# One list scheduler for a whole arm of an mLSTM and top-1 expert kernel

## The chip, the cores and the metric

The kernel runs on one core of a Trainium2 chip. A core has five engines with a queue each, which work in order and wait for each other on semaphores: TensorE (PE, with its weight loads shown apart as PEld), VectorE (DVE), ScalarE (ACT), GpSimd (POOL) and SyncE (SP), which here issues nearly all DMAs. The metric is the device time of one execution in microseconds; a smaller one is better.

## The reference

Two layers follow one another. The first is an mLSTM over 4 batches, 8 heads and 768 steps with head size 40. Each head keeps a 40 x 40 matrix state:

```python
m_new = np.maximum(f_gate[:, :, t] + m, i_gate[:, :, t])
f_stab = np.exp(f_gate[:, :, t] + m - m_new)
i_stab = np.exp(i_gate[:, :, t] - m_new)
C = f_stab * C + i_stab * outer(vt, kt)
n = f_stab * n + i_stab * kt
y[:, :, t] = sigmoid(o_gate[:, :, t]) * (C @ qt) / maximum(abs(n @ qt), 1)
```

The second takes the 3072 rows of 320 numbers and sends each to one of 8 experts, the one with the largest `x @ w_gate + modality_bias[modality_id]`; its output is `gate_w * (relu(x @ w1[e]) @ w2[e])` with a hidden size of 1024. All data is fp32. The large products are made of fp16 high and low parts.

## The kernel before

**Units.** The sequence is cut into 24 units, a batch and 128 steps each. `begin` computes the gates and a flag that says whether the state still moves after the first 128 steps of a batch; where it doesn't, the arm `still_state` runs, as it does in the runs shown, and otherwise the arm `general`. In `still_state` the first unit of each batch is "heavy": exponents on PE (`e`), their exp on ACT, scores on PE (`s`), and the product on DVE; it also gives the batch's state (`kw` on POOL, `up` on PE, `bd` on DVE). The other 20 units are "light": one product of q with the state (`values_l`). Every unit then has a denominator (`den`, DVE), an output gate (`so`, POOL; the logistic function before it, `sig`, is three ACT steps per half batch), the product (`row`, DVE), a sum of absolute values for scaling (`sum`, ACT) and an indirect store to the DRAM table `x_d` (`store`, POOL).

**Tiles.** The store puts a row where its modality says: rows of modality 0 from the front, those of modality 1 from the back. So 256 rows in a row ("tile") have one modality, and nearly all of them want the expert that the modality's bias alone would choose. Twelve such tiles go through that guessed expert (`deal`, six per modality, the weights of both kept on chip). A tile is loaded from `x_d` (SP), scaled and split into fp16 parts ("columns", ACT and DVE), turned by a DMA transpose (SP), and multiplied: layer 1 is four groups of 16 matmuls (`p`), each with a ReLU into a high part (`hh`, ACT) and a low part (`hl`, DVE); layer 2 is two halves of 128 rows with 24 matmuls each (`o`), a scaling (ACT) and an indirect store of the output (POOL). The first two tiles need five units, the next two nine, and so on.

**Gates, lists, rest.** The true logits of a tile are computed as well (`verify`, 16 small matmuls and some DVE steps). Rows that want another expert are masked in the output and put on lists in DRAM (`lists`). `work_list` turns these into "rest" tiles, of which two with 128 rows are done at the end (`slots`), with other weights: loaded, split into fp16 parts by ACT (`high`) and DVE (`low`), and the rows gathered by an indirect DMA.

**What sets the order.** The program order is written by hand (`manual_schedule`). Up to the second tile it comes from the class `Order`: tasks with an engine, a cost in us, what they come after, and the buffers they take; `give` walks forward in time, on each engine takes the task that can start first (within 0.2 us, the one with the longest way to the end), and emits the code in that order. It holds 12 units, the columns of four tiles, the weights of the two guessed experts, and the first two tiles; `FILL` warm-up matmuls go into PE's idle time. All the rest is done by eight generators ("threads") that `together` lets do one step each in turn, once per half of a quarter of a tile's matmuls (a half-beat): `light` (the 12 other units), `load_work`, two `column_work`, `weight_work`, `verify_work`, `list_work`, `rest_work`. Between them they wait for counts of half-beats, such as

```python
while now - max(turned[k, j] for k in range(NMOD) for j in js) < 2:
    yield
```

A thread that gives DVE more work than `FULL` elements in one half-beat makes patient threads wait (`Meter` counts them). The two rest tiles come after all threads are done.

Lines that the text below names: 1165 layer 1 on PE, 1169 and 163 its `hh` and `hl` (all DVE instructions carry line 163, the `Meter`'s), 1194 layer 2, 966 the output store, 943 the load of a tile, 997 the transpose, 954 the gather, 1667 `so`, 574 `store`, 1678 and 1685 the read-out of light and heavy units, 456 and 441 scores and exponents, 881 and 886 the weights' loads, 899 their `high`.

## Time and profile before

| | us |
|---|---|
| three runs | 280.53, 282.58, 283.46 |
| their median | 282.58 |
| the profiled execution | 280.47 |
| its span, first to last instruction | 278.8 |
| PE busy | 244.7 |
| DVE, ACT, POOL busy | 163.4, 126.9, 97.0 |

The mean granted TensorE clock is 0.952 of full speed. 41.20 MB go through the DMA engines, most of them in the first 90 us. In the profile a row of the groups reads: line, engine, operation, output <- inputs, shapes, count, then the busy time in us and the mean of one in ns, then the engine's idle time before such instructions and what ended it. A row of the timeline reads: start and length in us, engine, line, operation, and in square brackets the idle time before it and what ended that. A tile's busy time on PE can be read from the matmuls' starts; single matmuls overlap.

### The profile page before, as it was taken

The numbers are of one execution on the slowest core, as the hardware profiler recorded it, in microseconds if no ns is written. First come the engines' busy times: TensorE is split into PE (matmuls) and PEld (weight loads), VectorE is DVE, ScalarE is ACT, GpSimd is POOL, SyncE is SP. The second block draws the span as 40 slices with busy tenths as digits, with TensorE's granted clock in tenths as the row PEclk, the third lists the DMA queues.
The fourth block names the chain that finished last, engine by engine and source line by source line (L and its number), as shares of the span: only waits on it lengthen the run. The fifth ranks groups of instructions, "written<-read, shape, count | busy, mean of one in ns | idle before, by whom it ended". The sixth has DMA issues, their size and how long they took to land. (4 is left out here: it accounts for less than half of the span.)

```text
span 278.8 us, 6063 instructions
## 1 busy us (share of the span) xinstructions
PE 244.7 (88%) x2191; PEld 198.5 (71%) x2191; DVE 163.4 (59%) x572; ACT 126.9 (46%) x230; POOL 97.0 (35%) x159
## 2 busy tenths in 40 slices
PE   8984968999889999999999998999999989919930
PEld 3554854987768988879788886888787858708820
DVE  5886855885781465754857277656454756863200
ACT  4687562768742163824624353523131326772200
POOL 8275642253644136254453704021112214110110
PEclk9999587999999999999999999999999999986995
DMA  4985876997848004793351728881000068891000
GB/s 150 304 263 133 224 279 222 226 310 288 278 112 230 32 25 136 218 153 106 101 143 45 198 56 195 137 162 46 26 26 23 25 201 273 241 286 24 3 12 1
DMA packets 36666, 41.20 MB, mean 148 GB/s; under 512 B 23879, under 2 KB 27945, under 8 KB 36626
## 3 DMA queue, kind: packets, MB, share of 16 engines
q1 hardware_dynamic: 33650, 32.46, 43.2%
q0 software_dynamic: 2688, 8.23, 8.8%
q8 instruction: 19, 0.31, 0.5%
q14 instruction: 21, 0.17, 0.2%
q10 hardware_dynamic: 288, 0.03, 0.1%
HBM read 27.57 MB, written 8.55 MB: 130 GB/s over the span
## 5 line engine op out<-in xcount | busy, mean ns | idle before, releaser
L1165 PEld LDWEIGHTS <-wx 128*128 128x128 f16 x896 | 83.7, 100 | 18.5 <-DMA sg<-xr 7.1
L1194 PE MATMUL o_ps<-wx,hh 128*128 128x320 f16 x416 | 85.5, 299 | 0.0
L1165 PE MATMUL h_ps<-xT,wx 128*128 128x256 f16 x576 | 66.5, 272 | 2.3 <-DVE hl L163 2.3
L163 DVE SCALAR_TENSOR_TENSOR hl<-h_ps,hh 128x512 f16<-128x512 f32 x52 | 35.6, 687 | 50.6 <-ACT hh L1169 50.2
L1194 PE MATMUL o_ps<-wx,hl 128*128 128x320 f16 x208 | 62.2, 299 | 1.1 <-DVE hl L163 1.1
L1169 ACT ACTIVATE hh<-h_ps 128x512 f16<-128x512 f32 x52 | 30.8, 593 | 46.5 <-PE h_ps L1165 46.5
L1194 PEld LDWEIGHTS <-hh 128*128 128x128 f16 x416 | 39.9, 98 | 14.0
L966 POOL DMA_INDIRECT out<-ob,oi x24 | 25.1, 1045 | 69.3 <-ACT ob L965 65.1
L1667 POOL TENSOR_TENSOR so<-sg,den 128x320 f32<-128x320 f32 x24 | 20.5, 853 | 47.2 <-DVE den L163 39.5
L163 DVE SCALAR_TENSOR_TENSOR wx<-ws,wx 128x768 f16<-128x768 f32 (+1 forms) x24 | 27.8, 1157 | 11.8 <-ACT wx L899 11.5
L965 ACT ACTIVATE ob<-o_ps,entall 128x320 f32<-128x320 f32 x24 | 12.5, 523 | 46.6 <-PE o_ps L1194 38.7
L574 POOL DMA_INDIRECT x_d<-row,place_i x24 | 24.5, 1023 | 12.2 <-ACT ya L571 3.2
L1194 PEld LDWEIGHTS <-hl 128*128 128x128 f16 x208 | 20.3, 98 | 9.6 <-DVE hl L163 1.8
L899 ACT ACTIVATE wx<-ws 128x768 f16<-128x768 f32 (+1 forms) x24 | 23.3, 977 | 5.8 <-DMA ws<-in_w 5.8
L1678 PE MATMUL y_ps<-wx,eb 80*128 80x82 f32 x160 | 22.3, 288 | 2.4 <-DVE row L163 2.4
L1678 PEld LDWEIGHTS y_ps<-wx,eb 80*128 80x128 f32 x160 | 21.0, 206 | 3.1 <-issue 2.8
L1314 PE MATMUL warm_ps<-warm 128*128 128x512 bf16 x57 | 17.1, 464 | 6.0 <-DVE ah L163 3.6
L1165 PE MATMUL h_ps<-eb,wx 128*128 128x256 f16 x192 | 21.4, 273 | 0.0
L1314 PEld LDWEIGHTS <-warm 128*128 128x128 bf16 x57 | 6.5, 116 | 15.2 <-issue 10.3
L542 ACT ACTIVATE sg<-sg 128x960 f32<-128x960 f32 x16 | 15.8, 995 | 0.8 <-DMA sg<-in_og 0.7
L163 DVE SCALAR_TENSOR_TENSOR ex<-xg,sc,ex 128x64 f16<-128x64 f32 (+1 forms) x44 | 14.4, 378 | 0.9 <-ACT ex L989 0.9
L163 DVE TENSOR_TENSOR row<-y_ps,so 128x320 f32<-128x320 f32 x24 | 11.6, 482 | 5.5 <-POOL so L1667 5.5
(246 smaller groups left out, 259.0 us busy)
## 6 DMA issues: line engine op xcount, KB each, us to landing
ws<-in_w SPq DMA_DIRECT2D x16, 384.0 KB, 4.8
ws<-in_w SPq DMA_DIRECT2D x8, 640.0 KB, 7.7
xg<-x_d SPq DMA_DIRECT2D x14, 322.0 KB, 3.0
sg<-in_og SPq DMA_DIRECT2D x8, 480.0 KB, 5.5
eb<-in_ql SPq DMA_DIRECT2D x8, 320.0 KB, 5.7
kt<-in_kv SPq DMA_DIRECT2D x4, 324.0 KB
wx<-in_qk SPq DMA_DIRECT2D x8, 160.0 KB
eb<-in_ql SPq DMA_DIRECT2D x4, 160.0 KB, 2.3
```

Of the source, the lines that this page charges most:

```text
L163: return op(out, *args, **kw)
L542: nc.scalar.activation(t, t, AF.Exp, scale=-1.0)
L574: ins = nc.gpsimd.indirect_dma_start(out=x_d[:, :], out_offset=bass.IndirectOffsetOnAxis(ap=place_i[:, n:n + 1].bitcast(U32), axis=0), in_ ...
L899: nc.scalar.mul(halves[p][0], pieces[p], WSC)
L965: nc.scalar.mul(ob, o_ps, fac)
L966: disjoint("out", nc.gpsimd.indirect_dma_start(out=out[:, :], out_offset=bass.IndirectOffsetOnAxis(ap=oi.bitcast(U32), axis=0), in_=ob, in ...
L1165: nc.tensor.matmul(h_ps[:, i], lhsT=l, rhs=r, start=(i == 0 and q == 0), stop=(i == g - 1 and q == 7), skip_group_check=True)
L1169: nc.scalar.activation(hh[:, f0:f0 + g, 0:n], made[f0], AF.Relu)
L1194: nc.tensor.matmul(o_ps, lhsT=l[:, fc, hs], rhs=r[:, fc], start=(fc == 0 and a == 0), stop=(fc == NFC - 1 and a == 2))
L1314: nc.tensor.matmul(ps, lhsT=warm[:, 0:P], rhs=warm, start=True, stop=True, skip_group_check=True)
L1667: nc.gpsimd.tensor_tensor(sos[n], sgs[n // SGH][:, n % SGH].rearrange("p (h d) -> p h d", h=H), dens.pop(n).broadcast_to([P, H, D]), ALU.mult)
L1678: nc.tensor.matmul(y_ps[:, 2 * p:2 * p + 2], lhsT=qat[n][0:2 * D, p], rhs=bds[n // NCH][0:2 * D, p], start=(p == 0), stop=(p == NP - 1), s ...
```

## The change

`Order` now holds everything that the arm does: all 24 units, the columns of the twelve tiles and of the two further ones that are only verified, their gates and lists, the work list, the rest rows' gather, columns and weights, and all fourteen tiles; `first_work` becomes `all_work`, `first_tile` becomes `add_tile`, and the threads, the half-beats and the `Meter` are gone. These parts are changed with it:

- A task's way to the end counts the hop between engines (`HOP`, and `DEEP` behind PE), an added distance (`more`), order-only relations (`then`) and hints. Costs and latencies have new values. Only SP's DMAs wait for the modelled DMA line.
- Layer 1 of a tile comes after layer 1 of the tile before it and layer 2 of the one before that, so it may go ahead of the previous tile's layer 2. From the third tile on its groups go through the banks `psS`, `psS`, `psM`, `psS` where two `psS` banks (later `psS` and `psG`) served before.
- The first eight units use the banks of `psG` and `psS` by turns; before, all used the two of `psG`.
- Output scaling and output store are separate tasks (`scaled`, `send`).
- The idle filler is 12 matmuls of 128 columns (`keep_warm`, into a corner of a bank in use) at 0.8 us distance, until the first tile; before, 4 of 512 columns.
- `begin` now also issues a q group, the second half of the gates of batch 0 and the step constants, and does POOL's remaining constants, the padding and a zeroing that the arm did.

```diff
-FILL = 4
+FILL = 12
...
-    HOP = 0.12
+    HOP = 0.15
+    DEEP = 0.3
     NEAR = 0.2
-    WRITTEN = 2.2
-    LANDED, RATE = 1.7, 300e3
-
+    LANDED, RATE = 2.1, 300e3
     AHEAD = 0.7
...
+    def give(self, loaded, line, idle):
+
+
+        order, _, last = self.forth(loaded, line, idle, self.ways(loaded))
+        for _, _, do in order:
+            if do:
+                do()
+
+    def ways(self, loaded):
+
+        behind, then = ({n: [] for n in self.all} for _ in range(2))
+        for n, t in self.all.items():
+            for d, i in ((behind, "after"), (behind, "hint"), (then, "then")):
+                for a in t[i]:
+                    if a not in loaded:
+                        d[a].append(n)
         way = {}
 
         def back(n):
             if n not in way:
                 t = self.all[n]
-                way[n] = 0.0
-                way[n] = t["c"] + t["lag"] + (t["size"] / self.RATE + self.LANDED if t["size"] else 0) + max(
-                    [back(m) for m in behind[n]], default=0.0)
+                way[n] = t["c"] + max([back(m) for m in then[n]] + [
+                    t["lag"] + t["more"] + (t["size"] / self.RATE + self.LANDED if t["size"] else 0.0) +
+                    max([back(m) + self.hop(n, m) for m in behind[n]], default=0.0)])
             return way[n]
 
-        behind = {n: [] for n in self.all}
-        for n, t in self.all.items():
-            for a in t["after"]:
-                if a not in loaded:
-                    behind[a].append(n)
         for n in self.all:
             back(n)
-        free, end, line = {}, dict(loaded), 0.0
+        return way
+
+    def hop(self, a, b):
+        a, b = (self.all[n]["e"] if n in self.all else "" for n in (a, b))
+        return 0.0 if a == b else self.DEEP if a == "PE" else self.HOP
...
-                at = max([free.get(t["e"], 0.0)] + [end[a] + (self.HOP if engine.get(a) != t["e"] else 0) for a in t["after"]])
-                if t["size"]:
+                at = max([free.get(t["e"], 0.0)] + [end[a] + self.hop(a, n) for a in t["after"]])
+                if t["size"] and t["e"] == "SP":
...
+    def keep_warm(count):
+
+        ps = ubank[:, 512 - P:]
+        for _ in range(count):
+            nc.tensor.matmul(ps, lhsT=warm[:, 0:P], rhs=warm[:, 0:P], start=True, stop=True, skip_group_check=True)
...
+        pad_qk(1)
+        run_all(more_constants())
...
+        load_ql(0, 3, 2)
+        sgs.append(load_o(1))
+        load_steps_c(0)
...
+            for i, n in enumerate(U):
+
+                y, bank = (("s", (psS, "s")) if i < 8 and i % 2 else ("g", (psG, "g")))
                 r = [x for x, (b, c, k) in enumerate(qgroups) if b * NCH + c <= n < b * NCH + c + k]
                 if n % NCH:
-                    add(f"v{n}", "PE", 0.95, lambda n=n: values_l(n), [f"bd{n // NCH}", f"q{r[0]}"], [("g", f"row{n}")])
+                    add(f"v{n}", "PE", 0.95, lambda n=n, bank=bank: values_l(n, bank), [f"bd{n // NCH}", f"q{r[0]}"], [(y, f"row{n}")])
                 else:
-                    add(f"v{n}", "PE", 1.8, lambda n=n: values_h(n), [f"w{n},0", f"w{n},1"] + ([f"kv{n // NCH}"] if n else []), [("g", f"row{n}")])
+                    add(f"v{n}", "PE", 1.8, lambda n=n, bank=bank: values_h(n, bank), [f"w{n},0", f"w{n},1"] + ([f"kv{n // NCH}"] if n else []), [(y, f"row{n}")])
...
+                add(f"store{n}", "POOL", 1.05, lambda n=n: store_x(n), [f"sum{n}", "place"], size=165e3)
...
+            free_w = ([], ["s12,0", "s12,1", "s18,0", "s18,1"], all_v + [f"e{NCH * b},{hf}" for b in range(B) for hf in range(2) if b or hf],
+                      [f"o{done},1,1"])
...
+            head = deal + [(k, NST) for k in range(NMOD)]
...
+                    [f"store{n}" for n in range(UNITS[j])] + (["plan2"] if x else []), [("xg", f"xl{x},1")], 330e3,
+                    more=10.0 if x > 1 else 0.0)
+                add_columns(x, tl, [f"load{x}"] + ([f"sc{x - 1}"] if x else []), NH)
...
+            for i, js in enumerate(sets):
+                g, ls = verify(gs[i], js[0] == NST), lists(gs[i])
+                xs = [head.index((k, j)) for k in range(NMOD) for j in js]
+                big = len(js) > 1
+                for y, x in enumerate(xs):
+                    add(f"lg{x}", "PE", 0.5, lambda g=g: next(g), [f"xt{x},{h}" for h in range(NH)] +
+                        ([f"lg{xs[y - 1]}"] if y else ["wgr"] + ([f"gate{i - 1},0"] if i else [])))
+                for d, c in enumerate((1.5, 1.6, 1.0) if big else (1.2, 1.25, 0.8)):
+                    add(f"gate{i},{d}", "DVE", c, lambda g=g: next(g), [f"gate{i},{d - 1}"] if d else [f"lg{xs[-1]}", "plan4"] +
+                        ([f"gate{i - 1},2"] if i else []) + ([f"list{i - 2},2"] if i > 1 else []))
+                for d, (e, c) in enumerate((("DVE", 0.8), ("PE", 0.3), ("DVE", 1.3), ("DVE", 1.0), ("POOL", 1.7))):
+                    add(f"list{i},{d}", e, c, lambda ls=ls, d=d: (next(ls), next(ls) if d == 0 else 0), [f"list{i},{d - 1}"] if d else
+                        [f"gate{i},2"] + ([f"list{i - 1},3"] if i else []), lag=3.5 if d == 4 else 0.0, more=3.0 if d == 1 else 0.0)
+                if i == 0:
+                    w.all["list0,4"]["after"].append("zeros")
...
+            for x, (k, j) in enumerate(deal):
+                add_tile(w, x, early_w[k], tls[k, j], k, f"gate{[j in js for js in sets].index(True)},2", x > 1)
+
+            gt = []
+            for q, (wts, tl) in enumerate(slots):
+                x = len(head) + q
+
+                def lists_of(q=q, tl=tl):
+                    gt.append(gather_steps(rest, (0, TS)[q], tl, 1))
+                    next(gt[q])
+
+                add(f"load{x}", "SP", 1.7, lists_of, ["work3"] + [f"list{i},4" for i in range(n_sets)] + ([f"load{x - 1}"] if q else []), size=10e3)
+                add(f"rows{x}", "POOL", 1.7, lambda q=q: next(gt[q]), [f"load{x}"], [("xg", f"xl{x},0")], 165e3)
+                add_columns(x, tl, [f"rows{x}", "work5"], 1, lambda q=q: run_all(gt[q]))
+                add_tile(w, x, wts, tl, 2 + q, "work5", True, 1)
+            loaded = {"q0": 0.0, "w0,0": 0.0, "o0": 0.0, "get0,0": 0.5, "get0,1": 1.8, "q1": 3.4, "o1": 5.4, "steps0": 6.7}
+            w.give(loaded, 4.8, (lambda: keep_warm(FILL), 0.06 * FILL, 0.8, "p0,0"))
...
+        def add_tile(w, x, wts, tl, k, gates, more, nh=NH):
+
+            hid, made, l1, obs = [], {}, {}, {}
+            names = "ssms" if more else "s"
+            pools = [dict(s=(psS, "s"), m=(psM, "misc"))[i] for i in names]
+            n = NW1 * nh // NH
+
+            order = list(w.last)
+            after = [f"p{c},{w.last[c][0]}" for c in order[-1:]] + [f"o{c},{w.last[c][1]},1" for c in order[-2:-1]]
 
             def layer(part, f0):
                 if not l1:
-                    l1.update(zip("gphl", layer1_parts(wts, tl, both, hid, h_pools[0:1])))
+                    l1.update(zip("gphl", layer1_parts(wts, tl, list(range(nh)), hid, pools)))
                 l1[part](f0)
 
             def second(h, i):
                 made[h] = layer2_part(wts, hid, h, i, made.get(h))
-                if h and i:
-                    used(tl)
-
-            for i in range(NW1):
-                f0 = i * NFC // NW1
-                w.add(f"p{x},{i}", "PE", 1.78, lambda f0=f0: layer("p", f0), [f"low{x},{i}"] + [f"xt{x},{h}" for h in range(NH)] +
-                      ([f"p{x},{i - 1}"] if i else [f"o{x - 1},1,1"] if x else []) + (["gate4"] if (x, i) == (1, 0) else []), [("s", f"hl{x},{i}")])
+
+            for i in range(n):
+                f0, z = i * NFC // n, NW1 // n
+
+                w.add(f"p{x},{i}", "PE", 1.78, lambda f0=f0: layer("p", f0), [f"low{k},{c}" for c in range(z * i, z * i + z)] +
+                      [f"xt{x},{h}" for h in range(nh)] + ([f"p{x},{i - 1}"] if i else after),
+                      [(names[i % len(names)], f"hl{x},{i}")])
+                if order and i == n - 1:
+                    w.all[f"o{order[-1]},0,0"]["hint"].append(f"p{x},{i}")
                 w.add(f"hh{x},{i}", "ACT", 0.62, lambda f0=f0: layer("h", f0), [f"p{x},{i}"])
                 w.add(f"hl{x},{i}", "DVE", 0.7, lambda f0=f0: layer("l", f0), [f"hh{x},{i}"])
-            for h in range(NH):
+            for h in range(nh):
                 for i in range(2):
                     w.add(f"o{x},{h},{i}", "PE", 1.65, lambda h=h, i=i: second(h, i),
-                          [f"low{x},{NW1 + i}", f"p{x},{NW1 - 1}"] + [f"hl{x},{c}" for c in range(2 * i, 2 * i + 2)] +
-                          ([f"o{x},{h},0"] if i else []) + ([f"o{x},0,1"] if h else []), [] if i else [("y", f"out{x},{h}")])
-                w.add(f"out{x},{h}", "ACT", 0.55, lambda h=h: write(made[h], tl["fac"][:, h:h + 1], tl["oi"][:, h:h + 1]),
-                      [f"o{x},{h},1", "gate4"])
-            w.add(f"free{x}", "none", 0.0, None, [f"o{x},1,1", f"gate{x}"])
+                          [f"low{k},{NW1 + i}", f"p{x},{n - 1}"] + [f"hl{x},{c}" for c in range(n * i // 2, n * (i + 1) // 2)] +
+                          ([f"o{x},{h},0"] if i else []) + ([f"o{x},{h - 1},1"] if h else []) + ([f"o{order[-1]},{w.last[order[-1]][1]},1"] + [f"out{order[-1]},{h}"] if order and not (h or i) else []), [] if i else [("y", f"out{x},{h}")])
+                w.add(f"out{x},{h}", "ACT", 0.55, lambda h=h: obs.update({h: scaled(made[h], tl["fac"][:, h:h + 1])}),
+                      [f"o{x},{h},1", gates], [("ob", f"send{x},{h}")], lag=0.6)
+                w.add(f"send{x},{h}", "POOL", 1.05, lambda h=h: send(obs[h], tl["oi"][:, h:h + 1]), [f"out{x},{h}"], size=165e3)
+            w.last[x] = n - 1, nh - 1
...
-        threads = [light(), load_work(), column_work(0), column_work(1), weight_work(), verify_work(), list_work(), rest_work()]
-        patient = {threads[6]: 6}
-        put_off = {}
...
```

394 lines of the change are left out of this document (103 added, 291 removed).

## The prediction

> **What bounds the kernel now.** I began with the page's head and then cut the span into stages by engine, because a mean over 278.8 us hides where TensorE is not the limit. The columns of the second fence are the stretch and its length, the busy time and instructions of PE, PEld, DVE, ACT and POOL, the granted TensorE clock, the busy share of the DMA engines and GB/s.
>
> ```profile
> span 278.8 us, 6063 instructions
> PE 244.7 (88%) x2191; PEld 198.5 (71%) x2191; DVE 163.4 (59%) x572; ACT 126.9 (46%) x230; POOL 97.0 (35%) x159
> ```
> ```profile
> 0.00:20.00 20.00, 17.26 (x101) 9.96 (x102) 15.19 (x51) 13.00 (x19) 11.64 (x50) 1.00 0.78 238
> 20.00:47.80 27.80, 19.86 (x103) 14.97 (x102) 18.53 (x51) 16.61 (x29) 13.84 (x20) 0.75 0.70 214
> 47.80:90.00 42.20, 39.87 (x373) 34.32 (x371) 27.54 (x78) 24.57 (x45) 18.66 (x24) 1.00 0.80 238
> 90.00:170.00 80.00, 78.87 (x754) 66.42 (x753) 46.98 (x193) 35.64 (x77) 32.25 (x46) 1.00 0.44 116
> 170.00:244.60 74.60, 73.10 (x694) 59.20 (x692) 46.40 (x188) 28.49 (x50) 17.43 (x17) 1.00 0.49 121
> 244.60:251.40 6.80, 0.06 (x2) 0.03 (x2) 4.55 (x8) 5.13 (x7) 1.18 (x1) 0.79 0.91 277
> 251.40:268.00 16.60, 15.68 (x176) 13.60 (x176) 4.21 (x5) 3.45 (x6) 1.01 (x2) 0.88 0.03 6
> 268.00:278.80 10.80, 0.00 (x0) 0.00 (x0) 0.00 (x0) 0.00 (x0) 0.95 (x1) 0.70 0.02 6
> ```
>
> From 47.8 to 244.6 us TensorE is busy 39.87 + 78.87 + 73.10 = 191.84 of 196.8 us, on useful work, at the full clock. No other engine comes near that. So in this middle only the 5.0 us of holes can be won; no order of the other engines shortens the matmuls themselves. What an order can win lies at the two ends: before 47.8 us, where TensorE waits for its first rows, and at 244.6, where it stands for 6.8 us. The last 10.8 us hold no engine work but one DMA issue; the change leaves them.
>
> Next, what TensorE waited for (total, times, longest):
>
> ```profile
> PE h_ps L1165 <- DMA sg<-xr: 6.7, 1, 6.7
> PE warm_ps L1314 <- DVE ah L163: 3.6, 1, 3.6
> PE y_ps L1678 <- DVE row L163: 2.4, 1, 2.4
> PE h_ps L1165 <- DVE hl L163: 2.3, 2, 1.2
> PE ubank L836 <- DVE over L163: 1.5, 1, 1.5
> PE o_ps L1194 <- DVE hl L163: 1.1, 2, 0.8
> ```
>
> The 6.7 is the hole before the rest tiles, whose transposed columns come late. The two waits for `hl` (2.3 and 1.1) and the one for `over` (1.5) together are 4.9 us, which is the middle's 5.0. The other two lie in the front, and only touch the sum through the first tile's start.
>
> **The front, step by step.** The first tile can't start before the rows of five units are stored, loaded back and turned into columns. The timeline shows that chain (start, length, engine, line):
>
> ```profile
> 17.86 0.72 POOL L1667 TENSOR_TENSOR so<-sg,den 128x320 f32<-128x320 f32 x1 [1.27 <-DVE plan L163]
> ...
> 28.41 1.97 PE L1678 MATMUL y_ps<-wx,eb 80*128 80x82 f32 x8 [2.38 <-DVE row L163]
> ...
> 34.84 0.99 POOL L574 DMA_INDIRECT x_d<-row,place_i  x1 [1.39 <-ACT ya L571]
> ...
> 39.50 0.43 SPq L943 DMA_DIRECT2D xg<-x_d  x1
> ...
> 44.58 1.12 DVE L163 SCALAR_TENSOR_TENSOR xr<-xg,sc,xr 128x64 f16<-128x64 f32 x2 [0.63 <-ACT xr L989]
> ...
> 48.13 1.34 SPq L997 DMA_TRANSPOSE xT<-xr  x1
> ...
> 53.04 3.22 PE L1165 MATMUL h_ps<-xT,wx 128*128 128x256 f16 x28
> ```
>
> The next fence has the price of one unit on POOL and the time from issue to landing (the last number of the three DMA rows). The first row gives minimum, median and maximum of `so` in ns; the next two end in count, total and mean.
>
> ```profile
> L1667 POOL TENSOR_TENSOR so<-sg,den x24: 717/729/1850, 17.9 to 152.7; 128x320 f32<-128x320 f32 x24
> ```
> ```profile
> L574 POOL DMA_INDIRECT x_d<-row,place_i x24 | 24.5, 1023 | 12.2 <-ACT ya L571 3.2 <-issue 2.8 <-DVE den L163 2.2
> L567 POOL IOTA row<- 128x1 int32 x24 | 3.1, 130 | 0.0
> ```
> ```profile
> x_d<-row,place_i POOLq DMA_INDIRECT x24, 3.4
> xg<-x_d SPq DMA_DIRECT2D x14, 322.0 KB, 3.0
> xT<-ex SPq DMA_TRANSPOSE x13, 2.7
> ```
>
> The fifth store is issued at 34.84 and lands about 3.4 later, at 38.2. The load goes out at 39.50: 1.3 us lost in SP's queue. First half's columns end at 44.58 + 1.12 = 45.70, 6.2 after the load. The transposes go out at 48.13, another 2.4 lost in SP's queue, behind loads that wait for buffers. The tile starts 4.9 later. So the path from the fifth store's issue is 3.4 + 6.2 + 4.9 = 14.5 us of necessary steps plus 3.7 us of queueing: 34.84 + 18.2 = 53.04.
>
> The change shortens this path in three places. First, output banks: units took turns on two `psG` banks, and the 2.38 us wait at 28.41 is for the row that frees one. The first eight units now alternate between `psG` and `psS`, four banks. Second, the loads that units 3 to 5 need (a q group, a gate half, the step constants) go out in `begin`, and POOL's constants and pads too. Before 20 us POOL was busy only 11.64 us, so the moved POOL work has room; if it hadn't, the first `kw` would be late by what overflows, at most about a microsecond. Third, the order follows the length of each task's path to the end, DEEP and HOP included, and not the path to the first two tiles only.
>
> What is the earliest fifth store? POOL needs 0.729 + 0.130 + 1.023 = 1.88 us per unit, 9.4 for five. From the first `so` at 17.86 the fifth store would end at 27.3 and be issued at 26.2. That is the floor. Plus 14.5 gives 40.7 for the first tile. The top is 53.04 as now. I take 44: nearer the floor, with 1.8 us of POOL waiting for `kw` and the steps' copy, and 1.5 of the 3.7 us of queueing left, since SP's queue stays one line in order and any blocked load still holds the transposes behind it.
>
> Not all of these 9.0 us are won. From 47.80 to 53.04 TensorE had been doing 5.2 us of attention work that the earlier tile now comes ahead of. It doesn't vanish. Some of it will fit into the front, where TensorE was idle or only kept warm; I put half, 2.6 us, behind the tile's start. Front: 9.0 - 2.6 = **6.4 us** won, between 0 (tile at 53) and 12.3 (tile at 40.7, nothing moved behind).
>
> **The middle.** `p` of the next tile may now go ahead of layer 2 of the last one, and from the third tile on uses three banks (`psS` twice, `psM`) in place of two. That removes the 1.1 us for `hl` in layer 2 and most of the 2.3 in layer 1, which could come back only in the second tile, on two banks still; the 1.5 for `over` should go too, because the list places the small matmul when its operand is due and not in the next half-beat. Against it: TensorE's program is now written from estimated times. Each read-out, logits, list and layer-1 task is put at the first moment at which the list believes it ready, with no "two beats later" of slack. If its operand is late, everything behind it on TensorE waits. For the middle of the run the list's beliefs are on the safe side: a tile load is given 1.3 + 330/300 + 2.1 = 4.5 us against 3.0 measured, a transpose 1.25 + 2.0 = 3.25 against 2.7. So I let 3.9 us of new waits come for the 4.9 that go: **1.0 us** won, between +4.5 and a loss without a clear bound, which is the second rival. The DVE work moved here stays under cover: DVE was busy 46.98 of 80 and 46.40 of 74.6 us.
>
> **The end.** These are the two rest tiles:
>
> ```profile
> 251.37 5.62 PE L1165 MATMUL h_ps<-sg,wx 128*128 128x128 f16 x64 [6.74 <-DMA sg<-xr]
> 260.08 3.74 PE L1165 MATMUL h_ps<-kt,wx 128*128 128x128 f16 x64
> ```
> ```profile
> 159.12 0.98 POOL L574 DMA_INDIRECT x_d<-row,place_i  x1 [0.30 <-issue]
> ...
> 233.30 1.09 POOL L954 DMA_INDIRECT xg<-x_d,li  x1 [0.30 <-issue]
> ```
>
> All rows are stored by about 162.5 (159.12 + 3.4), yet the rest rows are gathered only at 233.3. In between lie some six transfers of 2.7 to 3.4 us and, by my estimate from the stage table, 15 to 20 us of DVE and TensorE steps: 40 us of chain in 71 us. The difference is patience that the threads were given. A list by path length has no reason to wait so long, so the columns are there when the twelfth tile ends, and the 6.74 us go. The second weights of the rest still need a buffer that is free only two tiles before the end, some 27 us; their splitting takes less. The 5.62 us is the same 64 matmuls as the 3.74: the clock fell in the hole (0.79 in that stretch). That is another 1.9. End: 6.7 + 1.9 = **8.6 us**.
>
> **Sum.** 278.8 - 6.4 - 1.0 - 8.6 = 262.8 us of span. The profiled execution took 280.47 us, 1.67 more than its span: 264.5. The median of the three runs, 282.58, is 2.1 above the profiled one, so the median to expect is 266.6, and I say 266.5.
>
> **Rivals.**
>
> Transfers bound the front. The order wouldn't matter if the bytes can't come faster.
>
> ```profile
> 14.00:53.00 39.00, 29.99 (x192) 23.89 (x191) 26.62 (x84) 24.55 (x40) 18.85 (x43) 0.82 0.76 221
> 24.00:26.00 2.00, 0.76 (x6) 0.35 (x5) 1.73 (x7) 1.86 (x2) 0.19 (x1) 1.00 0.31 74
> 45.00:47.80 2.80, 2.80 (x10) 1.15 (x9) 1.28 (x4) 0.00 (x0) 0.22 (x1) 0.62 0.31 80
> ```
>
> For it: a mean share of 0.76 from 14 to 53 us, and the list reckons with 300 GB/s where 221 flowed, so it will believe weights to be there that are not. Against it: two stretches at 0.31, in which SP's queue stood, so the mean isn't a ceiling. With no gain in front the time is 266.5 + 6.4 = 273. Chance 0.13.
>
> Stalls in the middle, the one that ends slower. The list's program for TensorE has about 24 read-outs, 14 logits, 6 list and 4 state matmuls between the tiles, 48 joints with another engine. Each late operand stops the matmuls, since TensorE was full. To eat the whole gain of 16.0 us takes 0.33 us per joint; to be over 1% slower (285.4) takes 18.9 us, 0.39 per joint; at 0.5 it is 24 us and 290. For it: the stretch that such a list ordered before, up to the second tile, has all the waits of the table but the 6.7, 1.5 and 1.1. Against it: those are front waits for rows, and the list's latencies for the middle are above the measured ones. Chance 0.14, and 0.07 more for stalls that just cancel the gain (around 282).
>
> POOL is slowed by a denser DVE.
>
> ```profile
> 20.27 1.34 POOL L1667 TENSOR_TENSOR so<-sg,den 128x320 f32<-128x320 f32 x1
> ...
> 39.64 1.85 POOL L1667 TENSOR_TENSOR so<-sg,den 128x320 f32<-128x320 f32 x1 [3.81 <-DVE den L163]
> ```
> ```profile
> 39.47 1.44 DVE L163 SCALAR_TENSOR_TENSOR wx<-ws,wx 128x1280 f16<-128x1280 f32 x1
> ```
>
> The usual `so` takes 0.729, these two 1.34 and 1.85, and the second lies under a weight split on DVE that reads two SBUF tensors. If the new order lays such a split over each of the first five `so`, the fifth store is 5 x 1.12 = 5.6 us later than the floor, 31.8 and not my 28.0, and 3.8 us of the gain are lost: 270. The Trainium skill's GPSIMD Engine Reference, section "8. Key points", says that GpSimd shares its SBUF interfaces with VectorE and meets contention with DVE instructions in a 2-port mode or with two SBUF inputs. By that rule the front pays for packing DVE; the 1.85 agrees with it, the 0.729 of most `so` shows that it is not the rule's every case. Chance 0.08.
>
> The rest tiles stay late, because their chain is put behind everything with a longer path to the end: 266.5 + 8.6 = 275. Chance 0.06.
>
> **The numbers.** My own forecast keeps 0.52: 259 (tile at 40.7 and the holes gone) to 271. With the transfers (273), POOL (270) and the late rest (275), 0.79 lies faster by over 1%, below 279.7. About 1% is what a measurement of this kernel can tell from no change. The 0.07 of cancelling stalls lies within 1%, and 0.14 is slower. Range 259 to 280: it takes in the forecast's bounds and the three smaller gains, and leaves out most of the 0.21 of stalls.
>
> **What would show it.** First tile (layer 1, first `h_ps`) starting at 41 to 46 us; the fifth store at about 28; the clock at 1.00 from 20 to 45 us; no `hl` wait over 1 us from the third tile on; no wait for `xr` transposes before the rest tiles, and both their layer-1 groups at about 3.7 us. I am wrong if the first tile starts after 50, or if the holes of TensorE between its start and the last matmul come to more than 10 us.

## The result, and the profile after

| | us |
|---|---|
| kernel before, in the same series | 281.82 (280.53 to 283.46, four runs) |
| kernel after | 269.25 (268.29 to 269.98, four runs) |
| ratio | 0.955, 95% interval 0.948 to 0.961 |
| profiled execution after, and its span | 269.57, 267.8 |

The change makes the kernel 4.5% faster. (The ratio of `rest_late` below is taken over its undisturbed executions, and its profile is of a disturbed one.) The forecast was 266.5, 2.75 lower than measured, and the time lies in the range. The parts of the sum, though, did not come as forecast. First the head of the page of the kernel after.

```profile
span 267.8 us, 6314 instructions
...
PE 246.5 (92%) x2310; PEld 203.3 (76%) x2311; DVE 163.1 (61%) x572; ACT 127.6 (48%) x230; POOL 93.5 (35%) x159
```

The stages of the kernel after (columns as before: stretch and length, busy time and instructions of PE, PEld, DVE, ACT and POOL, granted clock, DMA share, GB/s):

```profile
20.00:47.80 27.80, 23.17 (x198) 21.12 (x198) 19.88 (x62) 17.23 (x35) 17.10 (x25) 0.82 0.67 212
47.80:90.00 42.20, 39.53 (x425) 34.68 (x421) 27.20 (x76) 27.15 (x45) 8.34 (x14) 0.96 0.84 232
90.00:170.00 80.00, 80.00 (x723) 67.29 (x723) 44.56 (x167) 32.91 (x70) 34.04 (x48) 1.00 0.47 114
170.00:230.00 60.00, 59.52 (x603) 48.80 (x601) 40.87 (x193) 21.97 (x42) 13.85 (x14) 1.00 0.45 117
230.00:245.00 15.00, 15.00 (x150) 11.81 (x149) 12.04 (x26) 9.58 (x14) 3.29 (x3) 1.00 0.80 223
```

And what TensorE waited for, in the kernel after (total, times, longest):

```profile
PE h_ps L1165 <- DMA xT<-ex: 2.7, 1, 2.7
PE ubank L1358 <- POOL kw L423: 2.4, 1, 2.4
PE warm_ps L1320 <- POOL warm L1380: 1.4, 1, 1.4
...
PE ubank L1021 <- DVE run L1105: 0.5, 1, 0.5
```

From 90 to 245 us TensorE now stands still for 0.48 us in all, the one wait for `run`. The waits for `hl` and `over`, 4.9 us before, are gone, and so is the 6.7 for the rest tile's columns. The next rows are the timeline of PE after: the first half of the first tile's layer 1, the layer 1 of both rest tiles, the last matmul.

```profile
54.87 5.33 PE L1165 MATMUL h_ps<-xT,wx 128*128 128x256 f16 x32 [2.65 <-DMA xT<-ex]
...
237.39 3.74 PE L1165 MATMUL h_ps<-eb,wx 128*128 128x128 f16 x64
...
245.85 3.74 PE L1165 MATMUL h_ps<-eb,wx 128*128 128x128 f16 x64
...
255.81 0.30 PE L1194 MATMUL o_ps<-wx,hl 128*128 128x320 f16 x1
```

The last matmul before the change was this one:

```profile
266.78 0.30 PE L1194 MATMUL o_ps<-wx,hl 128*128 128x320 f16 x1
```

So TensorE is done 11.0 us earlier, and the tail behind it is 11.7 us in both kernels. The 11.0 splits into the first tile, which starts 1.83 us *later* (54.87 against 53.04), the middle, whose holes fell from 4.9 to 0.5 (4.4 won), and the end, which won the hole of 6.74 and 5.62 - 3.74 = 1.88 of cold clock (8.6): -1.8 + 4.4 + 8.6 = 11.2. Two further terms nearly cancel. The first tile's first 32 matmuls took 5.33 us, at a granted clock of 0.70 to 0.73 from 54 to 60 us, against 3.66 us before: 1.7 lost. And less of the light units' read-outs (L1678) is left behind the tile's start, 12.8 us in place of 14.6: 1.8 won.

What kept the first tile late? Its chain in the kernel after, from the timelines of POOL, SP's queue and PE:

```profile
23.61 0.72 POOL L1714 COPY wx<-wx 128x640 int32<-128x640 int32 x1 [4.03 <-DMA wx<-bp_d]
...
26.52 1.16 POOL L568 DMA_INDIRECT x_d<-row,place_i  x1 [0.66 <-issue]
...
35.29 1.03 POOL L568 DMA_INDIRECT x_d<-row,place_i  x1 [0.15 <-POOL row L561]
```
```profile
44.81 2.33 SPq L937 DMA_DIRECT2D xg<-x_d  x2
48.05 1.20 SPq L875 DMA_DIRECT2D ws<-in_w  x2
49.81 1.34 SPq L997 DMA_TRANSPOSE xT<-xr  x1
```
```profile
SPq L937 <- DMA x_d<-row,place_i: 28.6, 6, 13.9
```
```profile
44.68 7.53 PE L1315 MATMUL ubank<-warm 128*128 128x128 bf16 x132
```

The fifth store goes out at 35.29, not earlier than before (34.84). On the way to it the fifth unit's row waited 2.48 us on DVE for the transfer of an earlier store, since the rows have four buffers:

```profile
32.77 0.49 DVE L1672 TENSOR_TENSOR row<-y_ps,so 128x320 f32<-128x320 f32 x1 [2.48 <-DMA x_d<-row,place_i]
```

Three more things in these rows are set by the order in which the code stands, and not by a duration. POOL's copy of the step constants (L1714) waits 4.03 us for a load that writes a padded part (`part1`) and stands ahead of it in the program. The load of the first tile's rows, which needs five stores, waits up to 13.9 us in SP's queue, because the list had put two further stores ahead of it: all stores that stand before a load of `x_d` in the program have to land before it starts (`loads_ahead` below tests this). And 132 fill matmuls, 7.53 us, stand in PE's queue ahead of the first tile.

### The profile page after: what moved, and what is told of

Same layout as the page of the kernel before. It is cut to its first block, busy times and chain, and to the rows that moved or that the text cites. A ratio compares the mean times of both kernels' runs of the same rounds, so it can differ in the third digit from the quotient of the medians.

```text
span 267.8 us, 6314 instructions
## 1 busy us (share of the span) xinstructions
PE 246.5 (92%) x2310; PEld 203.3 (76%) x2311; DVE 163.1 (61%) x572; ACT 127.6 (48%) x230; POOL 93.5 (35%) x159
## 4 chain that ended last, share of the span: by engine, by line
PE 60%; DMA 13%; issue 12%; DVE 4%; POOL 4%; SPq 2%; ACT 1%; POOLq 0%; ACTq 0%; DVEq 0%
PE h_ps L1165 28%; PE o_ps L1194 22%; PE y_ps L1678 6%; DMA ws<-in_w 3%; DMA x_d<-row,place_i 3%; POOL out L966 2%; PE ubank L1021 2%; DMA wx<-in_steps_c 2%; DMA xT<-ex 1%; PE y_ps L1685 1%; DMA mb_sb<-in_mb 1%; DMA li<-list_d 1%; PE ubank L1358 1%; SPq L875 1%; DMA wx<-gp_d 1%
## 5 line engine op out<-in xcount | busy, mean ns | idle before, releaser
L1165 PEld LDWEIGHTS <-wx 128*128 128x128 f16 x896 | 82.7, 99 | 13.1 <-DMA xT<-ex 2.8
L1165 PE MATMUL h_ps<-xT,wx 128*128 128x256 f16 x512 | 60.0, 277 | 2.7 <-DMA xT<-ex 2.7
L1173 DVE SCALAR_TENSOR_TENSOR hl<-h_ps,hh 128x512 f16<-128x512 f32 x52 | 34.7, 683 | 23.4 <-ACT hh L1169 23.2
L966 POOL DMA_INDIRECT out<-ob,oi x24 | 24.1, 1003 | 65.4 <-ACT ob L962 63.1
L1667 POOL TENSOR_TENSOR so<-sg,den 128x320 f32<-128x320 f32 x24 | 18.4, 766 | 31.0 <-DVE den L1663 22.7
L565 ACT ACTIVATE ya<-row 128x320 f16<-128x320 f32 x24 | 11.2, 465 | 23.5 <-DVE row L1672 20.2
L1165 PE MATMUL h_ps<-kt,wx 128*128 128x256 f16 x192 | 22.1, 272 | 0.0
L1678 PE MATMUL y_ps<-wx,eb 80*128 80x82 f32 x160 | 21.7, 290 | 0.2 <-DVE wx L1650 0.2
L1678 PEld LDWEIGHTS y_ps<-wx,eb 80*128 80x128 f32 x160 | 20.6, 206 | 0.9 <-DVE wx L1650 0.6
L993 DVE SCALAR_TENSOR_TENSOR ex<-xg,sc,ex 128x64 f16<-128x64 f32 (+1 forms) x44 | 16.2, 418 | 2.0 <-ACT ex L989 2.0
L989 ACT ACTIVATE ex<-xg,sc 128x320 f16<-128x320 f32 x22 | 11.6, 552 | 5.5 <-DVE sc L987 5.2
```

What stands on the lines that cost most here:

```text
L966: disjoint("out", nc.gpsimd.indirect_dma_start(out=out[:, :], out_offset=bass.IndirectOffsetOnAxis(ap=oi.bitcast(U32), axis=0), in_=ob, in ...
L993: vec.scalar_tensor_tensor(xrs[h][:, o:o + z - a], xg[:, h, a:z], sc[:, h:h + 1].bitcast(F32), xrs[h][:, a:z], ALU.mult, ALU.subtract)
L1165: nc.tensor.matmul(h_ps[:, i], lhsT=l, rhs=r, start=(i == 0 and q == 0), stop=(i == g - 1 and q == 7), skip_group_check=True)
L1173: vec.scalar_tensor_tensor(hl[:, sl, 0:n], made.pop(f0), 0.0, hh[:, sl, 0:n], ALU.max, ALU.subtract)
L1667: nc.gpsimd.tensor_tensor(sos[n], sgs[n // SGH][:, n % SGH].rearrange("p (h d) -> p h d", h=H), dens.pop(n).broadcast_to([P, H, D]), ALU.mult)
L1678: nc.tensor.matmul(y_ps[:, 2 * p:2 * p + 2], lhsT=qat[n][0:2 * D, p], rhs=bds[n // NCH][0:2 * D, p], start=(p == 0), stop=(p == NP - 1), s ...
```

## The experiments

They ran in three series, each on a chip of its own beside the kernel before, so ratios to that are compared (its medians were 280.75, 283.15 and 281.11). Only differences that lie outside the intervals are read.

**First series: the front, and the order of the layers.** `loads_ahead` moves the code of the first two tile loads ahead of the sixth store; the order within each queue stays.

```diff
-        for _, _, do in order:
+        dos = [do for _, _, do in order]
+        for n, m in (('load0', 'store5'), ('load1', 'store5')):
+            dos.remove(self.all[n]["do"])
+            dos.insert(dos.index(self.all[m]["do"]), self.all[n]["do"])
+        for do in dos:
```

> The changed kernel with the code of the loads of the first two tiles put ahead of the sixth unit's store in the program; no queue's own order changes, only what the load must wait for. Theory A (the load waits for every store that stands before it in the program, seven and not five): the first load leaves when the fifth store has landed, about 39 us and not 44.8, and its transposes are out by 45; the first tile then starts right behind the warm-up matmuls that stand before it on TensorE, at about 52.2 and not 54.9; 2 to 3 us off the time. Rival B (the loads are late because the DMA engines are full): the load goes out earlier and lands later, first tile at 54 to 55, no gain.

Measured 269.27 us, ratio 0.957 (0.952 to 0.962): no gain over 0.955. The load did leave 4.2 us earlier (SP's queue and DVE in `loads_ahead`):

```profile
40.63 1.84 SPq L941 DMA_DIRECT2D xg<-x_d  x2
```
```profile
45.10 1.48 DVE L901 SCALAR_TENSOR_TENSOR wx<-ws,wx 128x1280 f16<-128x1280 f32 x1
46.50 0.68 DVE L468 SCALAR_TENSOR_TENSOR ah<-ah,s_ps 128x512 f32<-128x512 f32 x1
47.10 1.49 DVE L901 SCALAR_TENSOR_TENSOR wx<-ws,wx 128x1280 f16<-128x1280 f32 x1
48.50 0.16 DVE L986 CAST tok<-xg 128x2 f32<-128x2 int32 x1
```

But DVE, whose order was made for a later load, first did two weight splits and an attention product, and touched the rows only at 48.50. The first transpose left at 50.33, no earlier than the 49.81 of the kernel after, and the tile started at 54.73. The wait had only moved one queue further.

`no_fill` takes the fill out, alone; `loads_ahead_no_fill` together with the move.

```diff
-            w.give(loaded, 4.8, (lambda: keep_warm(FILL), 0.06 * FILL, 0.8, "p0,0"))
+            w.give(loaded, 4.8, (lambda: keep_warm(FILL), 0.06 * FILL, 1e9, "p0,0"))
```

> The changed kernel without the warm-up matmuls between tasks (those of the beginning stay). Theory A: they cover idle time only; the first tile stays at about 54.9, bound by its rows, and runs its first 3 to 4 us at the half clock, so 1 to 2 us are lost. Rival C (the warm-up matmuls stand in TensorE's queue in front of attention work and delay the rows): the fifth store and the first tile come 1 to 3 us earlier and the time is equal or shorter.

> Both edits of the two kernels before. Theory A: the first tile starts at about 49, 10 us after its load as in the changed kernel, since no warm-up matmul stands before it; less 2 us for the half clock, 3 to 4 us off the time. Rival B: no earlier than 54, and 1 to 2 us lost. Rival D (the weights of the second expert are late, so that an earlier first tile only waits behind itself): first tile at 49, but new waits for weights on TensorE before 80 us that eat most of it, within 1 us of the changed kernel.

`no_fill`: 273.51 us, ratio 0.968 (0.961 to 0.975). `loads_ahead_no_fill`: 270.82, 0.962 (0.957 to 0.967). Without the fill TensorE waits and is then cold, that is, it runs at a lower granted clock: 0.88 from 47.8 to 90 us in both, against 1.00 in `loads_ahead`, whose first 32 matmuls take 3.67 us (PE's first tile in `no_fill`, then in `loads_ahead_no_fill`):

```profile
56.69 5.53 PE L1165 MATMUL h_ps<-xT,wx 128*128 128x256 f16 x26 [10.31 <-DMA xT<-ex]
```
```profile
53.12 6.18 PE L1169 MATMUL h_ps<-xT,wx 128*128 128x256 f16 x32 [8.00 <-DMA xT<-ex]
```

With both edits the tile started at 53.12, and not at the 49 that I expected. The medians say that the fill is worth 1.6 us where the loads are ahead and some 3.6 (0.968 - 0.955) where not; the intervals overlap. It hides a wait that is there for other reasons.

`old_layers` holds layer 1 of a tile behind layer 2 of the tile before it, and gives it two banks:

```diff
-            names = "ssms" if more else "s"
+            names = "s"
...
-            after = [f"p{c},{w.last[c][0]}" for c in order[-1:]] + [f"o{c},{w.last[c][1]},1" for c in order[-2:-1]]
+            after = [f"o{c},{w.last[c][1]},1" for c in order[-1:]]
...
-                if order and i == n - 1:
-                    w.all[f"o{order[-1]},0,0"]["hint"].append(f"p{x},{i}")
```

> The changed kernel with layer 1 of a tile held behind layer 2 of the tile before it, and with two psS banks for all tiles. Theory A (the middle's gain comes from layer 1 ahead and from the third bank): the waits of layer 1 and 2 for hl come back, one or two of about 1 us in each tile without read-outs between its groups, some 10 us in all: 277 to 281. Rival E (it comes from the gates and lists being placed singly, and the layers' order doesn't matter while other work lies between): under 3 us lost, 269 to 272.

Measured 279.36, ratio 0.993 (0.989 to 0.996): most of the gain is gone. The waits of `old_layers` on PE:

```profile
PE o_ps L1194 <- DVE hl L1173: 2.8, 4, 1.6
...
PE h_ps L1165 <- DVE hl L1173: 2.2, 4, 1.2
```

The waits for `hl` are back, 5.0 us, of which the 2.8 of layer 2 all lie behind 245 us. But every path length changed with the edit, so the front is another one too (first tile at 59.10), and the two halves of the edit had to be tried apart.

**Second series.** `copy_ahead` puts the copy of the step constants ahead of the load that it waited for, by the same lines as `loads_ahead` with another pair:

```diff
+        for n, m in (('steps1', 'part1'),):
```

> The changed kernel with POOL's copy of the step constants put ahead of the load of a batch's parts into the copied tile; the queues' own orders stay. Theory F (the front's first domino is POOL: its copy waits 4.0 us for that load, which the list doesn't know, and all five stores, the key weighting and with it TensorE's attention stand behind it): the first store goes out at about 23.5 and not 26.5, the fifth at 32, the first tile starts at about 52; 2 to 3 us off the time. Rival G (the stores wait for ScalarE's sums, which stand behind the gates' steps): the copy is done by 21.5, but the first store stays at 26 or later and nothing is won.

Measured 274.6, ratio 0.971 (0.963 to 0.978), no gain. The copy ran at 19.53, 4.1 us earlier, and the first store went out as late as before (POOL in `copy_ahead`):

```profile
26.35 1.16 POOL L572 DMA_INDIRECT x_d<-row,place_i  x1 [2.94 <-ACT ah L1659]
```

Its row's sum was done at 22.4, its place at 17.4, so what held it is not its data. In every run but `old_layers` (30.3) the first store left between 25.8 and 28.0, the kernel before among them. What it waits for there stays open.

`front_all` makes three moves at once: both of the above, and the first tile's columns ahead of the fifth weight split on DVE. It halves the fill as well.

```diff
+        for n, m in (('steps1', 'part1'), ('load0', 'store5'), ('load1', 'store5'), ('sc0', 'low0,4'), ('xh0,0', 'low0,4'), ('xl0,0', 'low0,4'), ('xh0,1', 'low0,4'), ('xl0,1', 'low0,4')):
...
-            w.give(loaded, 4.8, (lambda: keep_warm(FILL), 0.06 * FILL, 0.8, "p0,0"))
+            w.give(loaded, 4.8, (lambda: keep_warm(FILL), 0.06 * FILL, 1.6, "p0,0"))
```

> The changed kernel with the copy ahead, the loads of the first two tiles ahead of the sixth store, the first tile's columns ahead of the last two weight splits on DVE and ScalarE, and half as many warm-up matmuls in TensorE's idle time. Theory F with H (each lever alone is taken back by the next queue: after the load it is DVE's, after that TensorE's warm-up matmuls): first tile at 47 to 49, 4 to 6 us off the time, 264 to 265. Rival B or D (bytes or the second expert's weights bound the front): first tile earlier, but new waits on TensorE before 80 us; 268 to 270.

Measured 273.7, ratio 0.965 (0.957 to 0.973). The first tile started 3.5 us earlier than in the kernel after, and no time was won (PE's first tile and two of its waits in `front_all`):

```profile
51.35 3.67 PE L1169 MATMUL h_ps<-xT,wx 128*128 128x256 f16 x32 [1.27 <-DMA xT<-ex]
```
```profile
PE h_ps L1169 <- DVE hl L1177: 2.7, 4, 1.4
PE ubank L1025 <- DVE run L1109: 1.5, 1, 1.5
```

Beside `copy_ahead`, on the same chip, the tile starts 4.8 us earlier (51.35 against 56.17) and the last matmul 0.2 us later (259.98 against 259.80). Holes behind the first tile took part of it back: 3.0 us before 90, for `hl` and for a transpose, where `copy_ahead` has none behind the tile's start. The two further holes, at 170.71 and 186.75 (0.80 and 1.47 us), are not this edit's: `copy_ahead` has them too (0.88 and 1.44).

`two_banks` is `old_layers`' first hunk alone: two banks, with layer 1 still allowed ahead.

```diff
-            names = "ssms" if more else "s"
+            names = "s"
```

> The changed kernel with two psS banks for layer 1 of all tiles; layer 1 stays ahead of the previous tile's layer 2, and the first 230 tasks of the order are the same. Theory J (the look-ahead does most, since a group that waits for its bank has layer 2 to go before it): under 2 us lost. Rival K (the third bank does it): waits for hl of 0.5 to 1.2 us come back in most tiles, 5 to 8 us lost.

Measured 278.49, ratio 0.981 (0.974 to 0.988). Beside the kernel after, on another chip, that says that the third bank is worth some 2%; beside `copy_ahead` (0.971), on the same chip, it is 1%, and the intervals overlap. The stages of `two_banks` show 1.67 + 3.36 = 5.0 us of holes from 90 to 245, where the kernel after has 0.5 and `copy_ahead` 2.6:

```profile
90.00:170.00 80.00, 78.33 (x698) 64.56 (x698) 41.39 (x163) 30.81 (x65) 33.00 (x45) 0.98 0.44 111
170.00:245.00 75.00, 71.64 (x698) 58.15 (x697) 51.67 (x222) 29.98 (x55) 18.43 (x19) 1.00 0.48 119
```
```profile
PE h_ps L1165 <- DVE hl L1173: 1.9, 2, 1.4
```

Only 1.9 us of these holes are waits for `hl`, for which the bank is there; both lie behind 170. The others wait for a read-out's operand (1.3), an output (0.8), `run` (0.5) and smaller things. So the expected wait in most tiles did not come, and how the bank brings its share is only in part shown.

`before_quick_rest` is the kernel before with the waits of its list and rest threads taken out, to see whether patience alone made the hole at the end:

```diff
-            for _ in range(4):
-                yield
...
-            for _ in range(2):
-                yield
...
-        patient = {threads[6]: 6}
+        patient = {}
```

> The kernel before with the patience taken out of the thread of the rest tiles: no waits for half-beats between the list's load, the gather and the columns, no delay of the lists thread under DVE load. Theory A (the hole before the rest tiles is the threads' patience): the 6.7 us wait shrinks below 3 us and the rest tiles' first group runs at the full clock; 5 to 8 us less than the kernel before, 274 to 276. Rival I (the rest's chain is that long in any order, for its DMAs and the second weights): the wait stays above 5 us, 280 to 282.

Measured 288.94, ratio 1.014 (1.005 to 1.023): slower than the kernel before. Its PE timeline and stages:

```profile
262.40 3.74 PE L1165 MATMUL h_ps<-sg,wx 128*128 128x128 f16 x64
```
```profile
90.00:170.00 80.00, 76.19 (x718) 63.80 (x716) 44.55 (x185) 34.16 (x73) 33.12 (x48) 0.98 0.39 109
170.00:245.00 75.00, 66.85 (x607) 51.68 (x606) 42.66 (x191) 23.13 (x45) 12.83 (x14) 0.93 0.44 98
```

The hole before the rest tiles is gone, and the first of them is at full clock. That alone shows little, since TensorE came to them 11 us later (262.40 against 251.37). What shows it is the first transpose of the rest rows: it left at 241.61, in the kernel before at 247.70, though the gather left only 0.65 us earlier (232.65 against 233.30). So the patience between gather and columns made most of the 6.74 us.

But TensorE now stands for 3.81 + 8.15 us between 90 and 245. The longest of these waits comes from the same edit (DVE, then PE):

```profile
236.84 0.16 DVE L163 CUSTOM_DVE_ANT_0 oir<-xg,padis 128x2 uint16<-128x2 uint16 x1 [5.65 <-DMA xg<-x_d,li]
```
```profile
239.32 0.71 PE L1194 MATMUL o_ps<-wx,hh 128*128 128x320 f16 x2 [4.37 <-ACT hh L1169]
```

DVE, and ScalarE behind it, stood in line for the gathered rows, which had not landed, and a tile's `hh` stood behind the rest rows' columns. The patience that made the hole had also kept these steps out of the way. The other waits were not taken apart.

**Third series.** `after_again` is the kernel after, unchanged.

> The changed kernel as it is, once more, beside the others of this series. If the runs on another chip and at another time compare by their ratios to the kernel before, this gives 0.955 again, within 0.945 to 0.965, with the first tile at 54 to 56 us. If chips weigh differently on the front (its clock and its transfers), the ratio is 0.97 or more, and then copy_ahead, front_all and two_banks, which ran beside each other on another chip, have cost less than their ratios say.

Measured 271.04, ratio 0.963 (0.959 to 0.968), which overlaps the first interval. So up to about 1% may lie between series, and `loads_ahead`, `no_fill`, `loads_ahead_no_fill`, `copy_ahead` and `front_all` are not told apart from the kernel after. In this profile the first tile starts at 56.98, 2.1 us later than in the first one of the same kernel, so start times in the front are not read closer than that.

`no_lookahead` is `old_layers`' other hunks alone (the hint goes too): layer 1 behind layer 2, with three banks.

```diff
-            after = [f"p{c},{w.last[c][0]}" for c in order[-1:]] + [f"o{c},{w.last[c][1]},1" for c in order[-2:-1]]
+            after = [f"o{c},{w.last[c][1]},1" for c in order[-1:]]
```

> Layer 1 of a tile again comes after layer 2 of the tile before it, with the three banks (psS, psS, psM, psS) kept. Theory L (the look-ahead is what fills TensorE between the tiles): the waits for hh and hl at the joints come back, some 0.8 us at each of ten joints, 6 to 9 us over the changed kernel, as in old_layers. Rival B (the third bank is what matters, as two_banks, which lost about 2.5% with the look-ahead kept, suggests): with three banks the order alone costs 0 to 3 us, and no wait for hl in layer 1 passes 1 us.

Measured 278.12, ratio 0.989 (0.982 to 0.997), 2.6% over `after_again`. The loss is not in the middle: TensorE is busy for 80.00 of 80 us and 59.56 of 60 from 90 to 230. It is at the end (PE in `no_lookahead`):

```profile
245.99 5.37 PE L1165 MATMUL h_ps<-eb,wx 128*128 128x128 f16 x64 [2.72 <-DMA eb<-xr]
259.16 0.30 PE L1194 MATMUL o_ps<-wx,hh 128*128 128x320 f16 x1 [0.96 <-ACT wx L893]
260.69 0.30 PE L1194 MATMUL o_ps<-wx,hh 128*128 128x320 f16 x1 [1.23 <-DVE wx L897]
262.78 0.30 PE L1194 MATMUL o_ps<-wx,hh 128*128 128x320 f16 x1 [0.30 <-DVE wx L897]
```

A hole of 2.72, 1.63 of cold clock, and 2.49 for the rest's weights: 6.8 us, against a last matmul that ends 6.4 later than in `after_again`. So with three banks the middle is full in either order. What the look-ahead brought shows at the rest tiles, whose rows this list gathers at 232.99, in `after_again` at 226.31. Why the list starts that chain later was not taken apart.

`rest_late` holds the first load of the rest's list until the first half of the eleventh tile's layer 2 is done:

```diff
-                add(f"load{x}", "SP", 1.7, lists_of, ["work3"] + [f"list{i},4" for i in range(n_sets)] + ([f"load{x - 1}"] if q else []), size=10e3)
+                add(f"load{x}", "SP", 1.7, lists_of, ["work3"] + [f"list{i},4" for i in range(n_sets)] + ([f"load{x - 1}"] if q else ["o10,0,1"]), size=10e3)
```

> The load of the first rest tile's list is held until the first half of layer 2 of the eleventh tile but one is done (o10,0,1), some 15 us later in the list; all before that is unchanged. Theory E (the end's gain of 8.6 us is the early rest chain and the warm clock that comes with it): a wait for the rest tile's transposed columns of 5 to 8 us comes back before its layer 1, that layer 1 takes more than 5 us in place of 3.7, and the time rises by 7 to 10 us, to a ratio of about 0.985. Rival: the rest chain runs faster than the list believes (transfers at 3 us, not 3.85 and more), so the hole is under 3 us and the time rises by less than 4.

Ratio 0.999 (0.994 to 1.004). Of the profile only the end is read (PE's timeline):

```profile
255.09 6.36 PE L1165 MATMUL h_ps<-eb,wx 128*128 128x128 f16 x64 [8.27 <-DMA eb<-xr]
262.91 3.74 PE L1165 MATMUL h_ps<-eb,wx 128*128 128x128 f16 x64
```

The rest rows are gathered at 239.77, 6.5 us later than in the kernel before, so the hole is longer than it was there. It is back with 8.27 us and the cold clock with 6.36 - 3.74 = 2.62, 10.9 together; by the ratios to `after_again`'s the edit costs (0.999 - 0.963) x 281.11 = 10 us. That a late chain of the rest rows costs this much is shown.

`front_full_fill` makes the moves of `front_all` and leaves the fill as it is:

```diff
+        for n, m in (('steps1', 'part1'), ('load0', 'store5'), ('load1', 'store5'), ('sc0', 'low0,4'), ('xh0,0', 'low0,4'), ('xl0,0', 'low0,4'), ('xh0,1', 'low0,4'), ('xl0,1', 'low0,4')):
```

> The three moves of front_all (the steps' copy ahead of the padded load, the first two tile loads ahead of the sixth store, the first tile's columns ahead of the fifth weight split), with the fill at its 0.8 us distance again. Theory W (what counts is TensorE's work before the first tile and the clock at which it is done, not the first tile's start): the clock from 20 to 48 us is back at 0.8, the first tile starts at 52 to 54 us behind the fill, and the time is within 2 us of the changed kernel. Rival F (the halved fill spoiled front_all): the first tile at 51 us now comes at the full clock, and the time is 3 to 4 us below the changed kernel, a ratio of 0.942.

Measured 266.64 us (265.53 to 268.97), ratio 0.947 (0.942 to 0.951). It is faster than both kernels: beside it, on the same chip, `after_again` took 270.38 to 271.81. The stage behind the front in `after_again` and then in `front_full_fill`, and the latter's first tile:

```profile
47.80:90.00 42.20, 38.23 (x423) 34.09 (x421) 26.74 (x67) 25.39 (x41) 7.04 (x13) 1.00 0.85 229
```
```profile
47.80:90.00 42.20, 41.82 (x474) 37.59 (x472) 30.28 (x80) 27.59 (x46) 9.80 (x16) 0.99 0.77 228
```
```profile
54.04 3.66 PE L1169 MATMUL h_ps<-xT,wx 128*128 128x256 f16 x32
```

The holes from 47.8 to 90 fall from 4.0 to 0.4 us. Neither of my two accounts of it holds. The tile does not start at 51, and the clock from 20 to 48 us is not back at 0.8, and yet the time falls. The columns are ready earlier (first transpose at 47.35 in place of 51.85 in `after_again`), so the 2.47 us wait ahead of the tile is gone, and with it one of 1.50 us for `hl` behind it. The last transpose leaves at 48.82 and takes some 2.6 us, so the columns are there at about 51.4; what holds the tile until 54.04 is now the fill. The profiled execution was the slowest of the four (268.97), and its last matmul starts 2.4 us before that of `after_again` (255.37 against 257.75): the profiles account for 2.4 of the 4.4 us between the medians. Why `front_all`, with the halved fill, did not gain is not settled: the chips differ too, and two of its holes stand in `copy_ahead` as well.

## Why the prediction was right or wrong

**The front, 6.4 us: wrong.** By my own mark (wrong if the first tile starts after 50) this step failed: the tile started at 54.87, and I had said 44. What failed is "I take 44: nearer the floor". The floor of 26.2 for the fifth store was made of POOL's durations, and of the 3.7 us of queueing on SP I took 2.2 off. Neither was the limit. Of the 10.9 us between 44 and 54.87, 7.3 lie ahead of the fifth store (35.29 in place of 28.0). The floor counted POOL's 1.88 us per unit from the first `so` on and no wait ahead of a store, but in the kernel before even the first store left only at 25.81. No run has the fifth store before 34.56 (`copy_ahead`). One piece of this is shown, the 2.48 us for a row buffer; what else holds the stores stays open. The other 3.6 us lie behind the fifth store (19.6 us in place of 16.0), in waits that the order of the code makes: load behind two later stores, columns behind weight splits. The moves against these and against the copy's wait gave 4.4 us together (271.04 to 266.64). Of the three, two were also run alone, on other chips, and gave nothing that their intervals show; the columns' move was not run alone. So the front had at least 4.4 us of the 6.4 to give, but not by this list, which does not know these waits. The 2.6 us of work that I put behind the tile's start did not come either: 1.8 us less stood there than before. I also took the start of the first tile as the measure of the front. `front_all` shows that it isn't: on one chip with `copy_ahead`, its tile starts 4.8 us earlier and its last matmul no earlier.

**The clock from 20 to 45 us at 1.00: wrong.** It was 0.82 from 20 to 47.8, and 0.75, as before the change, in `after_again`.

**The middle, 1.0 us: right in kind, mis-sized.** It won 4.4. The term that was off is the 3.9 us of new waits that I let come: 0.5 came. No wait for `hl` was left from the third tile on, as marked. The list's latencies for the middle were on the safe side, which may be why; no run changed them. I gave the gain to look-ahead and banks together. The runs lean to the third bank: with it the middle is full without the look-ahead (`no_lookahead`), and without it 5.0 us of holes come, of which 1.9 are waits for `hl` (`two_banks`).

**The end, 8.6 us: right.** The wait for the rest's columns is gone, both groups take 3.74 us, and `rest_late` brings the loss back. That the threads' patience made most of the hole is shown by `before_quick_rest`, where the rest rows' transpose left 6.1 us earlier. The gathers of the rest rows now stand at 224.36 and 228.54 against 233.30 and 234.70.

**The rivals.** Stalls in the middle: 0.5 us came of the 18.9 that it needed. The rest tiles stay late: no. Transfers bound the front: its outcome, no gain in front, came, but for another cause: in `front_full_fill` 233 GB/s flowed from 20 to 47.8 us, in the kernel after 212, so the transfers were no ceiling. POOL slowed by a denser DVE: one `so` in the front took 1.53 us, yet the mean fell from 853 to 766 ns (groups of the kernel after):

```profile
L1667 POOL TENSOR_TENSOR so<-sg,den 128x320 f32<-128x320 f32 x24 | 18.4, 766 | 31.0 <-DVE den L1663 22.7 <-DVE den L1661 7.9 <-DVE row L1672 0.2
```

**The sum.** Forecast 6.4 + 1.0 + 8.6 = 16.0 us off the span, measured 11.0. The front's 8.2 too much was partly made good by the middle's 3.4 too little, so the total came nearer than its parts deserved. I had also added 2.1 us from the profiled execution to the median; after the change the median lies 0.3 under the profiled one, which took 2.4 us more off the miss.

## What to carry to other kernels

Where an engine is full but for a few holes, add the holes up by place, and ask of each what order would fill it: here the end and the middle kept the promise. A list scheduler knows only the waits that it is told of; before trusting its start times for a chain through DRAM, ask what else stands ahead in the program and writes the same table or tile, and what the engines at the other end will be doing. One wait taken out of such a chain passes the time on to the next queue, so look at the whole chain before moving a link. All of it moved at once won 4.4 us in one form (`front_full_fill`) and nothing in another (`front_all`).

## What the runs showed of the hardware

For 18 us the clock did not come back with work. In `front_full_fill` TensorE was busy for 17.8 of 18 us from 26 to 44, and the granted clock stayed at 0.50 (stages of 3 us; the first and the last of the six, and the one after them):

```profile
26.00:29.00 3.00, 3.00 (x16) 3.00 (x15) 1.29 (x2) 2.94 (x6) 1.16 (x1) 0.50 1.04 256
...
41.00:44.00 3.00, 3.00 (x16) 2.77 (x15) 2.94 (x7) 2.30 (x7) 2.25 (x4) 0.50 0.65 169
44.00:47.00 3.00, 3.00 (x28) 2.91 (x28) 1.88 (x8) 2.62 (x7) 1.93 (x3) 0.93 0.91 248
```

The work there is mostly the fp32 attention matmuls. The Trainium skill's page "TensorE: Matmul & The Clock Gate", section "What's actually happening", says that about 3.4 us of sustained activity bring the full clock back. By that rule the half clock would have ended near 30; the rows do not agree, at least where "busy" is what this profile calls so. It came back from 44 us on (0.93), before the fill began at 46.67, while the last 24 score matmuls ran, which are fp32 as well. What counts as activity is open; in the fastest kernel these 18 us ran at half speed, so it is where the next gain may lie.
